# Pooled attention and a SOLU feed-forward on one core: wider loads and stores, and scores from every fourth token of a group

## The chip, the core and the metric

The kernel runs on one NeuronCore of a Trainium2 chip. Its engines work side by side, each through its own instructions in order: TensorE (PE, with PEld for its weight loads), VectorE (DVE), ScalarE (ACT), GpSimd (POOL), and SyncE (SP), which here only issues DMAs. The metric is the device time of one execution in microseconds (us), as the median of several runs.

## What is computed

Four batches of 12288 query tokens attend to 768 keys each. The keys are the means of 4x4 patches of `kv`, multiplied by a weight; they serve as values too. The result goes through a feed-forward layer with 1024 hidden units, a SOLU activation and a normalisation.

```python
r = 4
kv_pool = kv.reshape(B, H // r, r, W // r, r, C).mean(axis=(2, 4))
k = v = kv_pool.reshape(B, -1, C) @ w_sr            # 4 x 768 x 128
s = scale * (q @ k.transpose(0, 2, 1))              # 4 x 12288 x 768
a = np.exp(s - s.max(-1, keepdims=True))
a /= a.sum(-1, keepdims=True) + 1e-09
x = (a @ v).reshape(B * N, C)                       # 49152 x 128
...
h = x @ w_in                                        # 49152 x 1024
e = np.exp(h - np.max(h, axis=-1, keepdims=True))
solu = h * (e / (np.sum(e, axis=-1, keepdims=True) + 1e-09))
mu, var = mean and variance of solu over the last axis
return (((solu - mu) / np.sqrt(var + 1e-06) * g_ln) @ w_out)
```

## The kernel before

**Tiles and groups.** The 49152 tokens are 384 tiles of 128 tokens (`NT`), four tiles to a group (`GT`), 96 tiles to a batch (`TPB`). A tile's tokens lie on the 128 partitions for the scores, the hidden layer and the output. Queries arrive transposed (channels on partitions, tokens along the row), a group's 512 tokens at a time.

**Work of one tile.** Products are made from a high and a low part of each operand, so each matrix product takes three passes.

- Scores (`scores_pe`, line 402): the weights that PE loads are 128 columns of qh or ql, f32; kh and kl, 2x384 columns, stream past them: six loads and six matmuls. Line 398 picks the columns: tile j of a group takes columns j x 128 to j x 128 + 127. DVE takes the row maximum (419), ACT the exponential (420) and the high part (422), DVE the low part (430); SP issues a transposing DMA phl -> pT (433).
- Values (`values`, 456): 18 matmuls of 512 columns a group, spread over its tiles.
- Hidden layer (`hidden_pe`, 513): six matmuls of 512 columns. DVE (521, 554), ACT (537, 604) and POOL (578, 585) make u and split it into uhl; SP issues a transposing DMA uhl -> uT (589).
- Output (`final_pe`, 629): 24 weight loads from uT, 24 matmuls of 128 columns. Each group of four tiles is scaled by DVE (653) and stored by one DMA (662): its token j x 128 + p stands on partition p, so 512 bytes of a row of the output are one run.

**Keys.** A batch's keys are the sum of 16 patch positions. For batch 0 (`kv_first_load`, 163) they are loaded in 16 pieces of 384 KB and summed in PE. For batches 1 to 3 `kv_load` (204) loads one position, 384 KB, and `kv_add` (215) adds two halves of it on POOL. `kv_plan` lays these steps, and what makes keys and values of the sum, on slots of the batch before. The tiles are tag `kvc`, nine buffers of 3072 bytes a partition; other things (`vhl`, the last tiles' `uhl`) use the same tag.

**Queries.** `q_load` (373) loads one group, 256 KB, into one of three buffers, two groups ahead; `q_split` (382, ACT) makes the high part qh and `q_low` (390, POOL) the low part ql.

**Order.** The order is written by hand. The loop over `slot` (866 to 922) issues, for each slot, steps of several tiles at different stages: scores of tile slot + 1, the exponential of tile slot, the hidden layer of a tile ten slots back, the output of a tile thirteen slots back; `hidden_turn` of a tile comes eleven slots after its scores and `final_pe` two slots later. POOL's steps of the plan (`kv_add`) and SP's (`kv_load`) come at the end of a slot. All loads, stores and transposes go through SP's one queue in this order. Before the loop the loads of batch 0's keys, of both weights, of the first queries and of the first positions of batch 1 (`SOON`) are issued; the loop's table `SOON` also gave the slots of these positions' additions.

Of the kernel before, what the change touches and what calls it, by code (L numbers as in the profile page):

```python
# [11 lines left out]
F32 = mybir.dt.float32  # L12
F32R = mybir.dt.float32r
F16 = mybir.dt.float16
# [7 lines left out]
P = 128  # L22
B = 4
NTOK = 12288
NK = 768
RR = 16
DFF = 1024
# [4 lines left out]
GT = 4  # L32
# [22 lines left out]
IN_AT = 0  # L55
OUT_AT = 4

SOON = {0: (), 1: (-1, -1), 2: (8, 9), 3: (20, 22), 4: (24, 26), 5: (28, 30), 6: (32, 36)}
OUT0 = 6


# [1 line left out]
def kernel(  # L63
# [15 lines left out]
    nc = tc.nc  # L79

    dmt = ctx.enter_context(tc.tile_pool(name="dmt", bufs=2))
# [56 lines left out]
    state = {}  # L138
# [16 lines left out]
    def half_of(name, b, half):  # L155
        return state[name, b][:, half * 384 : half * 384 + 384]

    def kv_first_load(half, c):

        n = half * 8 + c  # L160
        tag, bufs = ("kvc", 9) if n < 9 else ("uT", 4) if n < 13 else ("uhl", 3)
        t = dmt.tile([P, 2, 384], F32, tag=tag, name=f"kv_{half}_{c}", bufs=bufs)
        nc.sync.dma_start(t, kv0[:, 2 * c : 2 * c + 2, half * 384 : half * 384 + 384])
        state["kv0", half, c] = t

# [31 lines left out]
        )  # L197
        nc.scalar.copy(half_of("kT", 0, half), pk)

    def kv_load(b, pos):  # L200

        t = dmt.tile([P, 2, 384], F32, tag="kvc", name=f"kv_{b}_{pos}", bufs=9)
        r, two = divmod(pos, 2)
        nc.sync.dma_start(
            t, kv[b - 1, r, :, two * NK : (two + 1) * NK].rearrange("p (h k) -> p h k", h=2)
        )
        state["kv", b, pos] = t

    def kv_add(b, half, pos):

# [108 lines left out]

    def kv_v_high(b, half):  # L320
        if half == 0:
            state["vhl", b] = dmt.tile([P, 2, NK], F16, tag="kvc", name=f"vhl_{b}", bufs=9)
        nc.gpsimd.tensor_scalar(
            state["vhl", b][:, 0, half * 384 : half * 384 + 384],
            half_of("ks", b, half),
            1.0,
            1.0,
            op0=ALU.mult,
            op1=ALU.mult,
        )  # L330
# [14 lines left out]
    def kv_plan(b):  # L345


        for pos in range(RR):


            if b == 1 and pos in SOON:
                for half, slot in enumerate(SOON[pos]):
                    yield slot, [partial(kv_add, b, half, pos)]
                continue

            n = pos - len(SOON) if b == 1 else pos
            slot = 12 * (n // 2) + 8 * (n % 2) + (7 if b == 1 else -37)
            yield slot, [partial(kv_load, b, pos)]
            if pos:
                yield slot + 3, [partial(kv_add, b, 0, pos)]  # L360
                yield slot + 5, [partial(kv_add, b, 1, pos)]
        for slot, part, *fs in PLAN:
            yield slot, [partial(f, b, part) for f in fs]


    QL = 1

    def q_load(g):
        if g >= NG or g % QL:
            return  # L370
        b, gb = divmod(g, GPB)
        t = dmt.tile([P, QL * 512], F32, tag="qf", name=f"qf_{g}", bufs=3)
        nc.sync.dma_start(t, qT[b, :, gb * 512 : (gb + QL) * 512])
        state["qf", g // QL] = t

    def q_split(g):
        if g >= NG:
            return
        qf = state["qf", g // QL][:, (g % QL) * 512 : (g % QL + 1) * 512]
        qh = grp.tile([P, 512], F32R, tag="qh", name=f"qh_{g}")  # L380
# [4 lines left out]
    def q_low(g):  # L385
        if g >= NG:
            return
        qf = state["qf", g // QL][:, (g % QL) * 512 : (g % QL + 1) * 512]
        qh, ql = state["q", g]
# [3 lines left out]
    def scores_pe(t):  # L393
        g, j = divmod(t, GT)
        b = t // TPB
        qh, ql = state["q", g]
        kh, kl = state["kh", b], state["kl", b]
        ts = slice(j * P, (j + 1) * P)
        s = ps_r.tile([P, 2, 512], F32, tag="r", name=f"s_{t}")
        for n, (lh, rh) in enumerate(((qh, kh), (qh, kl), (ql, kh))):  # L400
            for half in range(2):
                nc.tensor.matmul(  # L402
                    s[:, half, :384],
                    lh[:, ts],
                    rh[:, half * 384 : (half + 1) * 384],
                    start=n == 0,
                    stop=n == 2,
                )
        state["s", t] = s[:, :, :384]
        state["free", t] = s  # L410
# [154 lines left out]
    def hidden_high(t):  # L565
        u, _ = state["u", t]
        if t in LOW_DVE:
            uhl = [
                dmt.tile([P, DFF], F16, tag="kvc", name=f"uhl_{t}_{a}", bufs=9) for a in range(2)
            ]  # L570
            state["uhl", t] = uhl
        else:
            state["uhl", t] = dmt.tile([P, 2, DFF], F16, tag="uhl", name=f"uhl_{t}", bufs=3)
            uhl = [state["uhl", t][:, a, :] for a in range(2)]
        if t in HIGH_ACT:
            nc.scalar.copy(uhl[0], u)  # L576
        else:
            nc.gpsimd.tensor_scalar(uhl[0], u, 1.0, 1.0, op0=ALU.mult, op1=ALU.mult)  # L578
        state["halves", t] = uhl
# [69 lines left out]
    def final_out(g, j0=0, j1=GT):  # L649
        n = j1 - j0  # L650
        _, f = state["f", g]
        ob = dmt.tile([P, n, P], F32, tag="ob", name=f"ob_{g}_{j0}")
        nc.vector.scalar_tensor_tensor(
            ob,
            state["po", g][:, j0 * P : j1 * P].rearrange("p (j c) -> p j c", j=n),
            swi,
            f[:, j0:j1].unsqueeze(2).to_broadcast([P, n, P]),
            op0=ALU.mult,
            op1=ALU.mult,
        )  # L660
        t0 = g * GT + j0
        nc.sync.dma_start(
            out[t0 * P : (t0 + n) * P, :].rearrange("(j p) c -> p j c", p=P), ob
        )


# [27 lines left out]
    for n in range(16):  # L694
        if n == IN_AT:
            nc.sync.dma_start(raw_in, w_in.bitcast(I32))
        if n == 4:
            q_load(0)
        if n == OUT_AT:
            nc.sync.dma_start(raw_out, w_out.bitcast(I32))  # L700
        kv_first_load(*divmod(n, 8))
    if OUT_AT == 16:
        nc.sync.dma_start(raw_out, w_out.bitcast(I32))
    q_load(1)
    for pos in SOON:
        kv_load(1, pos)
    nc.scalar.mul(w_sr16, wsr, 1.0 / RR)

    wf, wr, in_steps = float64_parts(raw_in, "in")
# [95 lines left out]
    def w_low():  # L805
# [4 lines left out]
        1: [w_sum, partial(kv_norm_max, 0, 0)],  # L810
        2: [partial(kv_scale_v, 0, 1), partial(kv_scale_v, 0, 2), partial(kv_now, 0, kv_vs),
            partial(kv_now, 0, kv_v_high), partial(kv_now, 0, kv_v_low)],
        3: [partial(kv_norm_max, 0, 1), w_scale],
        4: [partial(kv_v_turn, 0, 0), w_in_low],
# [19 lines left out]
        (84, 0, kv_bound), (87, 1, kv_bound), (88, 2, kv_bound),  # L834
        (89, 0, kv_vs), (90, 1, kv_vs),
        (91, 0, kv_v_high), (92, 0, kv_v_low), (93, 1, kv_v_high), (94, 1, kv_v_low),
        (95, 0, kv_v_turn),
    ]
# [20 lines left out]
    for b in range(1, B):  # L859
        for k, fs in kv_plan(b):  # L860
            plan.setdefault((b - 1) * TPB + k, []).append(fs)
    for st in plan.pop(-1):
        st[0]()
    taken = []
    scores_pe(0)
    for slot in range(NT):

# [18 lines left out]
        if 0 <= av < NG:  # L886
            values(av, qtr, 0)
        at(slot + 1, scores_pe)
        for st in todo + [[partial(f, 0, 0) for f in (kv_norm_pe, kv_norm_out)]] * (slot == 4):
            if len(st) == 2:  # L890
                st[0](state["free", slot + 1])
                taken.append(st[1])
        at_soon(slot - NORM, values_norm)
        at_last(slot - FSC, final_scale)
        at(h0, hidden_high)
        at(h0, hidden_low)
        at_last(slot - FSC, final_root)
# [16 lines left out]
        if slot % GT == 0:  # L914
            q_load(slot // GT + 2)
        at_last(slot - LO - 1, final_out)
        at_soon(slot - XSP, values_out)
        for st in todo:
# [8 lines left out]
    for i in range(NT - LH, NT + 1):  # L927
        k = i - (NT - LH)
        if k in (0, XH):
            g = G - 1 if k == 0 else G  # L930
# [12 lines left out]
        if i - OB < LAST - GT:  # L943
            at_last(i - OB, final_out)
# [3 lines left out]
        if i < LAST:  # L948
            hidden_high(i - 1)
            hidden_low(i - 1)  # L950
            if i < LAST - 1:
                hidden_var(i - 1)
        elif i == LAST:
            hidden_high(i - 1)
            hidden_turn_half(i - 1, 0)
# [17 lines left out]
    final_scale(G)  # L973
    final_root(G)
    final_out(G - 1)
    for t in range(LAST - 1, LAST + 1):
        final_pe(t)
# [38 lines left out]
```

## Time and profile before

| | |
|---|---|
| median of 3 runs | 1879.23 us (1876.52 to 1888.96) |
| profiled execution | 1880.71 us, its span 1878.9 us |
| chain of work that ended last, by engine | PE 66%, POOL 11%, DVE 10%, issue 6%, DMA 4%, ACT 3% |
| DMA packets | 1483748, 434.43 MB; 1411472 of them under 512 bytes |
| HBM | 52.50 MB read, 25.17 MB written |
| L629 PEld, idle until DMA uT<-uhl | 35.3 us, 39 times |

The times of the prediction are made against the profiled execution. Busy time of an engine is a share of the span over stages with different limits; what a stage costs is read from a window of that stage. Rows of windows give the length of a window, then the busy time and the number of instructions (x) of each engine, the clock that TensorE was granted (1.00 is full), the share of the 16 DMA engines (overlapping packets count twice, so it goes above 1), and GB/s. Rows of waits give the engine and line that waited, what for, the total, the times and the longest. Rows of a timeline give start, length, engine, line, operation, the tile written and read, and how many instructions are merged.

### The profile page before, as it was taken

What the parts mean: (1) busy time and instruction counts of PE and PEld (TensorE: products, weight loads), DVE (VectorE), ACT (ScalarE), POOL (GpSimd) and SP (SyncE); (2) the same over time, 40 slices, a digit from 0 to 9 for tenths busy, and PEclk for the clock granted to TensorE, in tenths of its full rate; (3) what the DMA queues carried; (4) which work ended last, traced back from release to release, by engine and by line L of the source; (5) the groups of instructions that cost most, each with busy time, mean ns of one, the idle gap of its engine ahead of it and who ended that gap; (6) DMA issues with size and microseconds to landing.
All of it is one profiled execution on the core that took longest, in us unless ns stands there. A gap on an engine that the chain in (4) does not pass through costs nothing.

```text
span 1878.9 us, 43063 instructions
## 1 busy us (share of the span) xinstructions
PE 1837.0 (98%) x15676; PEld 1296.2 (69%) x15676; DVE 1787.7 (95%) x2692; ACT 1751.8 (93%) x3136; POOL 1630.9 (87%) x1400
## 2 busy tenths in 40 slices
PE   7899999999999999999999999999999999999997
PEld 5566777676676767767667767776677777777775
DVE  7899999999999999999999999999999999999996
ACT  4899999999999999999999999999999999999997
POOL 5899998999989888899988988888898888888886
PEclk9999999999999999999999999999999999999999
DMA  8999999999999999999999999999999999999998
GB/s 295 196 227 232 237 237 236 230 241 237 227 248 228 237 233 241 235 235 235 242 234 239 237 233 243 242 230 220 223 227 231 226 221 229 230 223 230 218 223 161
DMA packets 1483748, 434.43 MB, mean 231 GB/s; under 512 B 1411472, under 2 KB 1464848, under 8 KB 1483280
## 3 DMA queue, kind: packets, MB, share of 16 engines
q1 hardware_dynamic: 1483248, 431.60, 114.2%
q8 instruction: 124, 2.03, 0.5%
q14 instruction: 88, 0.72, 0.1%
q10 hardware_dynamic: 288, 0.07, 0.0%
HBM read 52.50 MB, written 25.17 MB: 41 GB/s over the span
## 4 chain that ended last, share of the span: by engine, by line
PE 66%; POOL 11%; DVE 10%; issue 6%; DMA 4%; ACT 3%; POOLq 0%; DVEq 0%; SPq 0%; ACTq 0%
PE o L629 19%; PE h L513 18%; PE s L402 15%; PE xa L456 14%; POOL uhl L585 4%; DMA uT<-uhl 3%; POOL uhl L578 3%; DVE junkd L521 2%; DVE nm L419 2%; DVE u L554 2%; DVE phl L430 2%; POOL ka L215 1%; DVE xl L472 1%; POOL ql L390 1%; ACT e L537 1%
## 5 line engine op out<-in xcount | busy, mean ns | idle before, releaser
L585 POOL TENSOR_TENSOR uhl<-u,uhl 128x1024 f16<-128x1024 f32 x382 | 815.7, 2136 | 33.5 <-ACT uhl L576 2.1
L629 PEld LDWEIGHTS <-uT 128*128 128x128 f16 x9216 | 545.0, 98 | 108.6 <-DMA uT<-uhl 22.5
L629 PE MATMUL o<-wch,uT 128*128 128x128 f16 x6144 | 577.2, 219 | 13.9 <-DMA uT<-uhl 12.8
L629 PE MATMUL o<-wcl,uT 128*128 128x128 f16 x3072 | 533.5, 219 | 0.0
L578 POOL TENSOR_SCALAR uhl<-u 128x1024 f16<-128x1024 f32 x377 | 394.8, 1047 | 150.8 <-DVE u L554 144.7
L554 DVE SCALAR_TENSOR_TENSOR u<-h,rz,e 128x1024 f32<-128x1024 f32 x384 | 491.3, 1279 | 29.3 <-ACT e L537 18.5
L521 DVE TENSOR_SCALAR_CACHE_REDUCE junkd<-h,rz 128x1024 bf16<-128x1024 f32 x384 | 491.1, 1279 | 4.6 <-PE h L513 4.1
L456 PE MATMUL xa<-pT,vT 128*128 128x512 f16 x1728 | 484.1, 381 | 1.7 <-DMA vT<-vhl 1.7
L537 ACT ACTIVATE e<-h,nm,rz 128x1024 f32<-128x1024 f32 x384 | 458.9, 1195 | 2.9 <-DVE junkd L521 2.9
L604 ACT ACTIVATE junk<-u,su 128x1024 bf16<-128x1024 f32 x384 | 438.1, 1141 | 0.2 <-DVE u L554 0.2
L419 DVE TENSOR_REDUCE nm<-s 128x1 f32<-128x768 f32 x384 | 364.9, 950 | 25.9 <-PE s L402 13.3
L420 ACT ACTIVATE s<-s,nm 128x768 f32<-128x768 f32 x384 | 335.4, 873 | 52.3 <-DVE nm L419 51.5
L430 DVE SCALAR_TENSOR_TENSOR phl<-s,phl 128x768 f16<-128x768 f32 x384 | 366.1, 953 | 2.5 <-ACT phl L422 2.5
L422 ACT ACTIVATE phl<-s 128x768 f16<-128x768 f32 x384 | 311.5, 811 | 14.1 <-DMA pT<-phl 2.0
L513 PEld LDWEIGHTS <-xh 128*128 128x128 f16 x1536 | 139.9, 98 | 198.3 <-DVE phl L430 31.7
L402 PE MATMUL s<-kh,qh 128*128 128x384 f32 x768 | 256.3, 415 | 9.4 <-DVE u L554 3.9
L456 PEld LDWEIGHTS <-vT 128*128 128x128 f16 x1728 | 139.5, 98 | 141.6 <-issue 57.1
L513 PE MATMUL h<-w_in_h,xh 128*128 128x512 f16 x768 | 228.7, 379 | 5.8 <-DVE phl L430 3.2
L513 PE MATMUL h<-w_in_h,xl 128*128 128x512 f16 x768 | 228.4, 379 | 0.0
L513 PE MATMUL h<-w_in_l,xh 128*128 128x512 f16 x768 | 228.4, 379 | 0.0
L402 PE MATMUL s<-kh,ql 128*128 128x384 f32 x768 | 197.0, 338 | 0.0
L402 PE MATMUL s<-kl,qh 128*128 128x384 f32 x768 | 195.1, 335 | 0.0
(121 smaller groups left out, 1686.2 us busy)
## 6 DMA issues: line engine op xcount, KB each, us to landing
kv<-in_kv_dram SPq DMA_DIRECT2D x64, 384.0 KB, 4.4
qf<-in_q_dram SPq DMA_DIRECT2D x96, 256.0 KB, 3.4
out_dram<-ob SPq DMA_DIRECT2D x95, 256.0 KB, 2.7
uT<-uhl SPq DMA_TRANSPOSE x386, 4.3
pT<-phl SPq DMA_TRANSPOSE x384, 4.0
raw_in<-in_moe_w_in_dram SPq DMA_DIRECT2D x1, 1024.0 KB, 5.2
raw_out<-in_moe_w_out_dram SPq DMA_DIRECT2D x1, 1024.0 KB, 8.0
out_dram<-ob SPq DMA_DIRECT2D x2, 128.0 KB, 1.8
```

The source lines that it names most:

```text
L402: nc.tensor.matmul(s[:, half, :384], lh[:, ts], rh[:, half * 384 : (half + 1) * 384], start=n == 0, stop=n == 2,)
L419: nc.vector.tensor_reduce(nm, s, axis=AX.XY, op=ALU.max, negate=True)
L430: nc.vector.scalar_tensor_tensor(phl[:, 1], state.pop(("s", t)), SC, phl[:, 0], op0=ALU.mult, op1=ALU.subtract)
L456: nc.tensor.matmul(xa, vT[:, v * NKC + c, :], pT[:, :, a * NKC + c, :], start=n == 0, stop=n == len(seq) - 1,)
L513: nc.tensor.matmul(h[:, hs], lh[:, ts], rh[:, hs], start=n == 0, stop=n == 2)
L521: nc.vector.tensor_scalar(junk, state["h", t], state["rz", g][1][:, j : j + 1], None, op0=ALU.mult, op1=ALU.min, accum_out=nm,)
L537: nc.scalar.activation(e, state["h", t], AF.Exp, bias=nm, scale=state["rz", g][0][:, js], accum_out=state["z2", g][:, js],)
L554: nc.vector.scalar_tensor_tensor(u, state.pop(("h", t)), state["rz", g][2][:, j : j + 1], state.pop(("e", t)), op0=ALU.mult, op1=ALU.mult, ...
L578: nc.gpsimd.tensor_scalar(uhl[0], u, 1.0, 1.0, op0=ALU.mult, op1=ALU.mult)
L585: engine.tensor_tensor(low, u, high, op=ALU.subtract)
L604: nc.scalar.activation(junk, u, AF.Square, scale=-float(DFF), bias=su, accum_out=state["v3", g][:, j : j + 1],)
L629: nc.tensor.matmul(po[:, ts], uT[:, a * NFC + c, :], w[:, c, :], start=start, stop=stop)
```

## The change

Four things change.

1. **A tile is every fourth token of its group.** `scores_pe` takes columns j, j + 4, j + 8, ... of qh and ql as weights, a step of four f32. Token 4p + j of a group then stands on partition p of tile j, from the scores to the output.
2. **The store** of a group writes the four tokens of a partition, which are neighbours in the output: 128 runs of 2048 bytes.
3. **Keys.** `kv_load` takes two positions at once, 768 KB, into five buffers of 6144 bytes a partition. Ahead of the loop four such loads (eight positions) are issued for batch 1. The plan is laid anew: batch 1's additions at slots 9 to 57, one or two slots apart; for batches 2 and 3 a load every twelve slots, its additions 2, 5, 8 and 11 slots later. Batch 0's pieces use the same tiles, two pieces to a tile.
4. **Queries.** `QL = 2`: one load of 512 KB for two groups, into one of two buffers.

```diff
-SOON = {0: (), 1: (-1, -1), 2: (8, 9), 3: (20, 22), 4: (24, 26), 5: (28, 30), 6: (32, 36)}
+SOON = 4
...
-        tag, bufs = ("kvc", 9) if n < 9 else ("uT", 4) if n < 13 else ("uhl", 3)
-        t = dmt.tile([P, 2, 384], F32, tag=tag, name=f"kv_{half}_{c}", bufs=bufs)
+        if n < 10:
+            if n % 2 == 0:
+                state["kv0", n] = dmt.tile(
+                    [P, 2, 2, 384], F32, tag="kvc", name=f"kv_{half}_{c}", bufs=5
+                )
+            t = state["kv0", n - n % 2][:, n % 2]
+        else:
+            tag, bufs = ("uT", 4) if n < 14 else ("uhl", 3)
+            t = dmt.tile([P, 2, 384], F32, tag=tag, name=f"kv_{half}_{c}", bufs=bufs)
...
-    def kv_load(b, pos):
-
-        t = dmt.tile([P, 2, 384], F32, tag="kvc", name=f"kv_{b}_{pos}", bufs=9)
-        r, two = divmod(pos, 2)
-        nc.sync.dma_start(
-            t, kv[b - 1, r, :, two * NK : (two + 1) * NK].rearrange("p (h k) -> p h k", h=2)
-        )
-        state["kv", b, pos] = t
+    def kv_load(b, r):
+
+        t = dmt.tile([P, 2, 2, 384], F32, tag="kvc", name=f"kv_{b}_{r}", bufs=5)
+        nc.sync.dma_start(t, kv[b - 1, r].rearrange("p (w h k) -> p w h k", w=2, h=2))
+        for w in range(2):
+            state["kv", b, 2 * r + w] = t[:, w]
...
-        for pos in range(RR):
-
-
-            if b == 1 and pos in SOON:
-                for half, slot in enumerate(SOON[pos]):
-                    yield slot, [partial(kv_add, b, half, pos)]
-                continue
-
-            n = pos - len(SOON) if b == 1 else pos
-            slot = 12 * (n // 2) + 8 * (n % 2) + (7 if b == 1 else -37)
-            yield slot, [partial(kv_load, b, pos)]
-            if pos:
-                yield slot + 3, [partial(kv_add, b, 0, pos)]
-                yield slot + 5, [partial(kv_add, b, 1, pos)]
+
+        for r in range(RR // 2):
+            slot = 12 * r - 42
+            if b > 1 or r >= SOON:
+                yield slot, [partial(kv_load, b, r)]
+            for n in range(4):
+                pos, half = 2 * r + n // 2, n % 2
+                if not pos:
+                    continue
+                if b > 1:
+                    at = slot + 3 * n + 2
+                elif pos == 1:
+                    at = -1
+                else:
+                    at = 9 + 9 * (4 * (r - 1) + n) // 5
+                yield at, [partial(kv_add, b, half, pos)]
...
-    QL = 1
+    QL = 2
...
-        t = dmt.tile([P, QL * 512], F32, tag="qf", name=f"qf_{g}", bufs=3)
+        t = dmt.tile([P, QL * 512], F32, tag="qf", name=f"qf_{g}", bufs=2)
...
-        ts = slice(j * P, (j + 1) * P)
+        ts = slice(j, GT * P, GT)
...
-        t0 = g * GT + j0
         nc.sync.dma_start(
-            out[t0 * P : (t0 + n) * P, :].rearrange("(j p) c -> p j c", p=P), ob
+            out[g * GT * P : (g + 1) * GT * P, :].rearrange("(p j) c -> p j c", j=GT)[:, j0:j1], ob
         )
...
-    for pos in SOON:
-        kv_load(1, pos)
+    for r in range(SOON):
+        kv_load(1, r)
```

More of the change, by code (lines that the diff above doesn't have):

```diff
@@ L321, in kv_v_high @@
         if half == 0:
-            state["vhl", b] = dmt.tile([P, 2, NK], F16, tag="kvc", name=f"vhl_{b}", bufs=9)
+            state["vhl", b] = dmt.tile([P, 2, NK], F16, tag="kvc", name=f"vhl_{b}", bufs=5)
         nc.gpsimd.tensor_scalar(
@@ L568, in hidden_high @@
             uhl = [
-                dmt.tile([P, DFF], F16, tag="kvc", name=f"uhl_{t}_{a}", bufs=9) for a in range(2)
+                dmt.tile([P, DFF], F16, tag="kvc", name=f"uhl_{t}_{a}", bufs=5) for a in range(2)
             ]
```

## The prediction

> **What bounds the kernel now.** I read the page's busy shares first, then equal amounts of work in different stages, then the chain of waits inside the quietest stage.
>
> ```profile
> span 1878.9 us, 43063 instructions
> PE 1837.0 (98%) x15676; PEld 1296.2 (69%) x15676; DVE 1787.7 (95%) x2692; ACT 1751.8 (93%) x3136; POOL 1630.9 (87%) x1400
> ...
> core 0: us, PE busy (x) PEld busy (x) DVE busy (x) ACT busy (x) POOL busy (x), PEclk, DMA share, GB/s
> 67.04:294.22 227.18, 223.26 (x1893) 156.30 (x1894) 216.52 (x320) 213.79 (x381) 208.86 (x179) 1.00 1.15 229
> 466.95:752.77 285.82, 282.05 (x2434) 199.08 (x2432) 274.02 (x406) 269.68 (x482) 254.62 (x217) 1.00 1.20 236
> 924.93:1208.03 283.10, 281.36 (x2434) 199.47 (x2432) 273.85 (x406) 269.66 (x482) 254.62 (x217) 1.00 1.20 238
> 1379.52:1660.02 280.50, 280.50 (x2434) 199.78 (x2432) 273.33 (x406) 269.39 (x482) 235.34 (x197) 1.00 1.15 227
> ```
>
> The busy shares alone decide nothing: four engines are near full. The four windows are cut at the first matmul of s of a tile. The last three each hold 60 tiles, tiles 0 to 59 of batches 1, 2 and 3, with the same 2434 matmuls; the first holds tiles 12 to 59 of batch 0. In batch 3 no keys are prepared, PE is busy 280.50 of 280.50 us, and a tile takes 280.50/60 = 4.675 us. DVE, ACT and POOL have idle time there, so PE alone sets this pace, at a granted clock of 1.00 and with the DMA engines' share above 1.
>
> ```profile
> 1444.86 0.30 PEld L402 LDWEIGHTS s<-kh,qh 128*128 128x128 f32 x2
> 1445.15 0.36 PEld L402 LDWEIGHTS s<-kl,qh 128*128 128x128 f32 x2
> 1445.50 0.36 PEld L402 LDWEIGHTS s<-kh,ql 128*128 128x128 f32 x2
> ...
> 1445.08 1.09 PE s L402 x6
> 1446.17 0.88 PE xa L456 x4
> 1447.05 1.29 PE h L513 x6
> 1448.35 1.34 PE o L629 x24
> 1449.69 0.22 PE xa L456
> ...
> 1440.75 1.04 PE s L402 x6
> ```
>
> The middle rows are the chain of waits for one tile in that stage: nothing but PE; the last is the tile before. Scores s, values xa, hidden h and output o follow each other without a gap. So whatever the change adds to a PE section is paid 384 times, and whatever it takes off the DMA queues is worth only PE's stalls elsewhere. At 4.675 us a tile, 48 tiles of batch 0 need 224.4 us. The stretches of batches 0 to 2 therefore lose 227.18 - 224.4 = 2.8, 285.82 - 280.5 = 5.3 and 283.10 - 280.5 = 2.6 us: 10.7 us in all.
>
> **The weight loads of s, read in strides.** The two multiplications with qh and the one with ql load six 128x128 f32 weights a tile. Today each partition reads 128 neighbouring f32; then it reads one f32 of every four, 16 bytes apart. The number and size of the matmuls stay. What matters is whether a slower load is still covered by the matmul before it.
>
> ```profile
> L402 PEld LDWEIGHTS s<-kl,qh x768: 186/188/331, 29.5 to 1824.1; 128*128 128x128 f32 x192
> ...
> 36.92 0.50 PEld L402 LDWEIGHTS s<-kh,qh 128*128 128x128 f32 x2 [1.20 <-PE s L402]
> ...
> 36.90:38.80 1.90, 1.85 (x6) 1.78 (x6) 1.87 (x5) 1.87 (x5) 1.23 (x2) 0.50 0.79 178
> ```
>
> The recorded 0.188 us of a load is not its cost, because loads overlap. The pairs of loads quoted above say more. In a pair of 0.36 us the second ends 0.19 us after its own start, so it started 0.36 - 0.19 = 0.17 us after the first: that is the matmuls' pace (1.04 to 1.09 us for six). The pair of 0.30 us, the first two loads of a tile whose preceding matmul is a short one of o, shows a load that nothing holds back: the next could start 0.30 - 0.19 = 0.11 us later. So a load needs about 0.11 us under a cover of 0.17.
>
> At a granted clock of 0.50 (last row) the free pair takes 0.50 us. Its second load is recorded at about 0.33 us, near the 331 ns maximum quoted, so the distance is about 0.165 us. My estimate from these two points: 0.165 - 0.11 = 0.055 us of a load is reading of columns at full clock, and 0.055 us is fixed. The half-clock row is also a direct picture of a load whose reading takes twice as long: 0.165 us, still under 0.17.
>
> No row shows a 16-byte step, so the cost is bounded. Lower end: nothing, 0 us; a gain is excluded, since PE runs at the matmuls' pace here. Upper end: today a 16-byte piece serves four columns, then one; if each piece costs what it costs now, reading takes 4 x 0.055 = 0.22 us and a load 0.275. Then five loads of a tile each add 0.275 - 0.17 = 0.105. The first, behind a 0.22 us matmul of xa in three tiles of four, adds 0.055, and behind a short one of o in the fourth 0.275 - 0.11 = 0.165. A tile pays 0.525 + 0.75 x 0.055 + 0.25 x 0.165 = 0.61 us, and 384 tiles 233 us. At twice the reading time only the fourth tile's first load shows: 0.25 x 0.055 x 384 = 5.3 us. The cover is gone at (0.17 - 0.055)/0.055 = 2.1 times.
>
> ```profile
> L712 DVE TENSOR_SCALAR ex_in<-ex_in 128x1024 int32<-128x1024 int32 x3 | 2.1, 691 | 0.1
> L712 DVE TENSOR_SCALAR ex_in<-raw_in 128x1024 int32<-128x1024 int32 x1 | 0.7, 694 | 4.7 <-DMA raw_in<-in_moe_w_in_dram 4.7
> ```
>
> The nearest strided row is DVE's: ex_in<-raw_in takes every second 32-bit word, 8 bytes apart, in 694 ns; the same operation on neighbouring words takes 691. Half-used pieces cost nothing there. It is another engine and half the step, so I take the lower part of the range: between no loss and twice the reading, **+3 us** (ends 0 and +233).
>
> The Trainium skill, Advanced Engine Details and Errata (Memory Cachelines, SBUF Cachelines), speaks against this: it puts SBUF lines at 16 bytes, wants at least two hits on a line to absorb the access latency, and names a penalty for a different line on each access. By it the DVE row (two hits, 691 against 694 ns) should be free, and the trace agrees; the one hit of the new loads no run here shows. It gives no size for PE. With the P / 1.2 of TensorE: Matmul & The Clock Gate (LDWEIGHTS (loading the stationary operand)), 107 ns for 128 columns, doubled to 213 as an estimate, a tile would pay about 0.24 us and the kernel about 92 us.
>
> **Stores of 2048 bytes.** A group's 512 tokens then lie four to a partition, so a store writes 128 runs of 2048 bytes instead of 512 of 512. The same bytes move, with fewer descriptors.
>
> ```profile
> kv<-in_kv_dram SPq DMA_DIRECT2D x64, 384.0 KB, 4.4
> qf<-in_q_dram SPq DMA_DIRECT2D x96, 256.0 KB, 3.4
> out_dram<-ob SPq DMA_DIRECT2D x95, 256.0 KB, 2.7
> ...
> PEld L629 <- DMA uT<-uhl: 14.2, 20, 1.8
> PE o L629 <- DMA uT<-uhl: 5.7, 10, 1.4
> ```
>
> Nobody waits for a store; its queue is shared with the transposes uT, for which PE waited 14.2 + 5.7 us between 160 and 1830 us (the two waits rows). Batch 3 does the same stores without a stall, so relief there is worth nothing. In the measured stretches at most the 10.7 us lost in batches 0 to 2 can return: ends -10.7 and 0. Most of that loss comes where keys are loaded and added, so I take **-4 us**.
>
> **Keys of two positions in a load.** 24 loads of 768 KB replace 48 of 384 KB for batches 1 to 3, and the additions keep their number and size. Batch 1's first eight positions are asked for ahead of the loop (seven today), and its remaining additions are spread over tiles 9 to 57; the four later loads are issued 24, 19, 15 and 10 tiles before their first addition, so POOL cannot wait for them unless they are very late. In batches 2 and 3 the first addition follows its load by two tiles instead of three, in seven pairs of eight (the first pair has eight).
>
> ```profile
> 647.32 0.57 SPq L204 DMA_DIRECT2D kv<-in_kv_dram  x1
> ...
> 656.84 1.01 POOL L215 TENSOR_TENSOR ka<-ka,kv 128x384 f32<-128x384 f32 x1
> ```
>
> From issue to first addition are 656.84 - 647.32 = 9.5 us today; one tile less leaves 4.85. Loads of 256 and 384 KB land after 3.4 and 4.4 us, so 768 KB after about 3.4 + 4 x 1.0 = 7.4 (estimate): each of 14 additions would hold POOL about 2.5 us, and behind it wait the splits of u into uhl, their transposes, and PE's o. POOL is idle 285.82 - 254.62 = 31.2 us in 60 tiles, 0.52 a tile, and 12 tiles lie between loads, so each delay is made good in some five tiles. Ends: 0 and 14 x 2.5 = +35 us; I take **+3 us**, a tenth, since o comes about two tiles after its transpose is issued and that slack takes most of it. Should the estimate of the landing be too long, the wait is gone altogether.
>
> **Queries of two groups in a load.** 48 loads of 512 KB for 96; they are issued five tiles before their first use, as now, and the two double buffers come free as early as the three single ones. In the loop nothing waits. At the start 256 KB more stand before 12 of batch 0's key loads:
>
> ```profile
> 5.96 11.43 SPq L163 DMA_DIRECT2D kv<-in_kv_dram  x12
> ...
> PE pk L179 <- DMA kv<-in_kv_dram: 7.1, 1, 7.1
> ```
>
> Twelve loads of 384 KB took 11.43 us, so 256 KB are 0.65 us. PE waited for these loads only once, before the first matmul, and that load is still ahead of the queries; taken 0, ends 0 and +0.65. SP issues 24 + 48 = 72 loads fewer at about 0.57 us, 41 us of its queue; since batch 3 runs with PE never waiting, taken 0.
>
> **Sum.** The profiled execution took 1880.71 us (span 1878.9 and 1.8 around it), against a median of 1879.23. 1880.71 + 3 - 4 + 3 = 1882.7, so 1883 us, 0.2% above the median. About 1% is what a measurement of this kernel can tell from no change (1860 to 1898).
>
> **The rivals.** *A load of s outgrows its cover* (slower). Place: the six loads of L402. It decides from 2.1 times the reading time on: 0.006 us over the cover on five loads, with the fourth tile's first load, is already 1%. For it: no gap in PE, so nothing absorbs it, and the step leaves a piece of 16 bytes with one use. (The rule of the Trainium skill's Advanced Engine Details and Errata, Memory Cachelines, quoted above, is this mechanism.) Against it: 0.165 us at twice the reading is still covered, and DVE's 8-byte step is free. Between 2.1 and 4 times it gives 1885 to 2114; its middle is 2000 us.
>
> *The wider key load is late at POOL.* All 14 waits reach PE: 1883 + 32 = 1915 us. For it: 4.85 us of lead against an estimated 7.4. Against: POOL's 0.52 us a tile, and o's distance from its transpose.
>
> *The DMA relief returns more than the stretches show:* the whole wait for uT, 14.2 + 5.7 = 19.9 us, goes: about 1861 us. Against: that sum includes delays that come from POOL, not from the queue.
>
> **How the numbers follow.** Forecast 0.46 (its own range 1868 to 1897); the load over its cover 0.44; the late key load 0.07; full relief 0.03. The range 1866 to 2050 leaves out the relief and those loads above 3.5 times the reading, 0.15. Faster by over 1%: the relief, 0.03. Slower: 0.41 of the covered-load rival (0.03 of it stays under 1898) and half the late key load, 0.45. Within 1%: the rest, 0.52.
>
> **What would show it.** If the loads are covered, batch 3's 60 tiles still take 280.5 us and six matmuls of s 1.04 to 1.09. If not, that row grows to 1.2 to 1.7 us, every other PE section keeps its length, and DVE, ACT and POOL get idle time. Pairs of loads of 0.30 us would read 0.36 at twice the reading. A late key load would show as POOL idle before L215's additions. The prediction is wrong if the s row grows by more than 0.05 us a tile, or if PE's stalls in batches 1 and 2 exceed today's 5.3 and 2.6 us by some ten.

## The result and the profile after

The changed kernel takes 1990.54 us (median, 1989.61 to 1991.51) against 1881.09 for the kernel before in the same runs: 1.0577 times as long, 95% interval 1.0558 to 1.0596. The point forecast, 1883 us, was wrong by 107 us and had the wrong verdict; the time lies inside the stated range because of the first rival.

The page of the changed kernel, its first lines and the chain that ended last:

```profile
span 1989.7 us, 42994 instructions
PE 1961.6 (99%) x15676; PEld 1468.0 (74%) x15676; DVE 1801.6 (91%) x2692; ACT 1757.1 (88%) x3136; POOL 1631.6 (82%) x1400
...
PE 95%; ACT 1%; DMA 1%; DVE 1%; issue 1%; POOL 0%; SPq 0%; POOLq 0%; DVEq 0%; ACTq 0%
PE s L409 26%; PE o L636 25%; PE h L520 24%; PE xa L463 19%; DMA kv<-in_kv_dram 1%; ACT e L544 0%; PE pk L186 0%; ACT junk L611 0%; DMA vT<-vhl 0%; DVE phl L437 0%; POOL kv L183 0%; DVE u L561 0%; PE s L226 0%; ACT uhl L583 0%; DVE junkd L528 0%
```

PE's share of the chain rose from 66% to 95%, and the scores are now its costliest line. The count of instructions on PE is unchanged, 15676. The same stretches as before, tiles 0 to 59 of batches 1, 2 and 3 (length, then busy time of PE, PEld, DVE, ACT, POOL, clock, DMA share, GB/s):

```profile
491.36:792.46 301.10, 301.10 (x2434) 226.37 (x2432) 275.99 (x406) 270.18 (x481) 253.59 (x215) 1.00 1.12 224
974.75:1275.85 301.10, 301.10 (x2434) 226.36 (x2432) 275.99 (x406) 270.18 (x481) 253.63 (x215) 1.00 1.13 225
1457.92:1759.02 301.10, 301.10 (x2434) 226.35 (x2432) 275.98 (x406) 270.18 (x481) 235.62 (x196) 1.00 1.04 212
```

Two things are to be seen. A tile takes 301.10/60 = 5.018 us instead of 4.675, 0.343 more, at the same granted clock. And all three stretches are equal to a hundredth: the stalls that batches 1 and 2 had before (5.3 and 2.6 us) are gone; between 160 and 1830 us the trace has no wait of PE for a transpose left. Over 384 tiles 0.343 us are 132 us; the spans differ by 1989.7 - 1878.9 = 110.8. About 21 us of stalls were given back. 12.6 of them lie in the stretches of the prediction: tiles 12 to 59 of batch 0 grew by 238.99 - 227.18 = 11.8 instead of 16.5 us, and the others by 15.3 and 18.0 instead of 20.6.

Where the 0.343 us are, in batch 3 (the weight loads of a tile that follows a short matmul of o, then the chain of the tiles around it):

```profile
1507.95 0.54 PEld L409 LDWEIGHTS s<-kh,qh 128*128 128x128 f32 x2
1508.40 0.56 PEld L409 LDWEIGHTS s<-kl,qh 128*128 128x128 f32 x2
1508.86 0.56 PEld L409 LDWEIGHTS s<-kh,ql 128*128 128x128 f32 x2
...
1503.52 1.36 PE s L409 x6
1504.87 0.66 PE xa L463 x3
1505.54 1.29 PE h L520 x6
1506.83 1.34 PE o L636 x24
1508.17 1.51 PE s L409 x6
1509.68 0.88 PE xa L463 x4
...
L409 PEld LDWEIGHTS s<-kl,qh 128*128 128x128 f32 x768 | 216.6, 330 | 0.0
```

Only the s row grew, from 1.04 and 1.09 us to 1.36 and 1.51; h, o and a matmul of xa keep their 1.29, 1.34 and 0.22. A load is recorded at 0.33 us (last row). So in the pair of 0.54 the second starts 0.54 - 0.33 = 0.21 us after the first, where it was 0.11: that is what a strided load needs when nothing holds it. In the pairs of 0.56 the distance is 0.23 us, where the matmuls' pace was 0.17. Five such distances, 0.06 us more each, and the first load's part (0.02 us behind a matmul of xa, 0.11 behind one of o) make the 0.34 us. Why the distance between the matmuls of s is 0.02 us longer than that of the unheld pair, no run shows.

### The profile page after: what moved, and what is told of

The parts are those of the page before. It is cut to its first block, busy times and chain, and to the rows that moved or that the text cites. A ratio compares the mean times of both kernels' runs of the same rounds, so it can differ in the third digit from the quotient of the medians.

```text
span 1989.7 us, 42994 instructions
## 1 busy us (share of the span) xinstructions
PE 1961.6 (99%) x15676; PEld 1468.0 (74%) x15676; DVE 1801.6 (91%) x2692; ACT 1757.1 (88%) x3136; POOL 1631.6 (82%) x1400
## 4 chain that ended last, share of the span: by engine, by line
PE 95%; ACT 1%; DMA 1%; DVE 1%; issue 1%; POOL 0%; SPq 0%; POOLq 0%; DVEq 0%; ACTq 0%
PE s L409 26%; PE o L636 25%; PE h L520 24%; PE xa L463 19%; DMA kv<-in_kv_dram 1%; ACT e L544 0%; PE pk L186 0%; ACT junk L611 0%; DMA vT<-vhl 0%; DVE phl L437 0%; POOL kv L183 0%; DVE u L561 0%; PE s L226 0%; ACT uhl L583 0%; DVE junkd L528 0%
## 5 line engine op out<-in xcount | busy, mean ns | idle before, releaser
L409 PE MATMUL s<-kh,qh 128*128 128x384 f32 x768 | 298.1, 470 | 4.4 <-DVE phl L437 2.6
L520 PEld LDWEIGHTS <-xh 128*128 128x128 f16 x1536 | 149.7, 98 | 183.5 <-DVE phl L437 2.9
L409 PE MATMUL s<-kl,qh 128*128 128x384 f32 x768 | 242.7, 398 | 0.0
L409 PE MATMUL s<-kh,ql 128*128 128x384 f32 x768 | 242.3, 398 | 0.0
```

What stands on the lines that cost most here:

```text
L409: nc.tensor.matmul(s[:, half, :384], lh[:, ts], rh[:, half * 384 : (half + 1) * 384], start=n == 0, stop=n == 2,)
L520: nc.tensor.matmul(h[:, hs], lh[:, ts], rh[:, hs], start=n == 0, stop=n == 2)
```

## The experiments

All ratios are to the kernel before, run beside it on the same chip.

**1. The strides alone.** In the kernel before, one line:

```diff
-        ts = slice(j * P, (j + 1) * P)
+        ts = slice(j, GT * P, GT)
```

> The kernel before with one line changed: scores take columns j, j + 4, ... as weights; the store stays as it was, so the rows of the output stand permuted within each group. Theory (the strided load alone makes the loss): two loads of s that nothing holds start 0.21 us apart instead of 0.11, the six matmuls of s keep 0.233 us instead of 0.172, a tile in batch 3 takes 5.02 us instead of 4.675, and the time is 1985 to 1995 us. Rival (half or more of the loss comes from the wider loads, the stores or the new plan): under 1940 us.

Measured: 1992.0 us (ratio 1.059, 1.0569 to 1.0612), the time of the whole change. Its stretches of batches 1 and 3:

```profile
489.51:790.61 301.10, 301.10 (x2434) 226.34 (x2432) 275.97 (x406) 270.19 (x481) 254.48 (x217) 1.00 1.10 226
1455.84:1756.94 301.10, 301.10 (x2434) 226.32 (x2432) 275.98 (x406) 270.17 (x481) 235.65 (x196) 1.00 1.05 212
```

The same 301.10 us, in batch 2 too. One line makes the loss; the loads, stores and plan add nothing beside it.

**2. The rest alone.** The changed kernel, with the permutation of tokens moved into the layout of the queries on the host:

```diff
-        ts = slice(j, GT * P, GT)
+        ts = slice(j * P, (j + 1) * P)
...
-        "q": inputs["q"].transpose(0, 2, 1),
+        "q": inputs["q"].reshape(B, GPB, P, GT, P).transpose(0, 4, 1, 3, 2).reshape(B, P, NTOK),
```

> The changed kernel with contiguous weights: the queries are laid out on the host with the tokens of a group in the order of the tiles, so tile j takes columns 128j to 128j + 127 and these still are every fourth token; stores, key loads, query loads and plan as changed. Theory (these parts are hidden): batch 3 runs at 4.675 us a tile again, and the time is 1868 to 1885 us, below the kernel before by at most the 11 us that its batches 0 to 2 lose. Rival (the late key load): 1890 to 1915 us, with POOL waiting for DMA before its additions in batches 1 and 2.

Measured: 1895.4 us (1.0087, 1.0056 to 1.0118), inside the rival's 1890 to 1915. The 95 us between this run and the changed kernel are the strides; the rest is not hidden either, but costs about 14 us where PE has its old pace. Batch 3 is back at 4.675 us a tile, batches 1 and 2 lose 9.2 and 9.9 us (5.3 and 2.6 in the kernel before), and new waits stand in the list (waiter, releaser, total us, times, longest):

```profile
470.13:759.84 289.71, 283.58 (x2434) 200.00 (x2432) 274.39 (x406) 270.12 (x483) 253.87 (x216) 0.99 1.19 232
1397.64:1678.15 280.51, 280.51 (x2434) 199.73 (x2432) 273.28 (x406) 269.18 (x482) 235.09 (x197) 1.00 1.13 228
...
POOL ka L220 <- DMA kv<-in_kv_dram: 20.3, 9, 4.1
PE xa L463 <- DMA pT<-phl: 12.2, 8, 2.8
```

How a wide load reaches PE, in one place (SP's queue, then POOL, then the chain of work that ended last):

```profile
685.60 0.57 SPq L210 DMA_DIRECT2D kv<-in_kv_dram  x1
686.27 1.39 SPq L440 DMA_TRANSPOSE pT<-phl  x1
687.76 5.02 SPq L596 DMA_TRANSPOSE uT<-uhl  x1
692.88 1.42 SPq L440 DMA_TRANSPOSE pT<-phl  x1
...
685.73 2.14 POOL L592 TENSOR_TENSOR uhl<-u,uhl 128x1024 f16<-128x1024 f32 x1
691.66 0.99 POOL L220 TENSOR_TENSOR ka<-ka,kv 128x384 f32<-128x384 f32 x1 [3.80 <-DMA kv<-in_kv_dram]
...
686.27 6.91 DMA pT<-phl
693.17 0.25 issue
693.42 1.65 PE xa L463 x4
```

POOL stands 3.80 us, until the load has landed at about 691.6. But PE's wait does not come from POOL. It ends with the transpose that was issued at 686.27, right behind the load: it lands after 6.91 us, where the median of these transposes is 3.9. All eight waits in the row of pT above are of this kind; the transpose behind the wide load landed 6.5 to 8.1 us after its issue. The next transpose, of uhl, then stays at the head of SP's queue for 5.02 us. POOL is not what holds it, since POOL's part of uhl was ready at 685.73 + 2.14 = 687.87. What does hold it is not shown; it moves on when the transpose before it has nearly landed.

**3. A step of two columns.** As the changed kernel, but tile j takes every second token of half a group:

```diff
-        ts = slice(j, GT * P, GT)
+        ts = slice(j // 2 * 2 * P + j % 2, (j // 2 + 1) * 2 * P, 2)
...
-            out[g * GT * P : (g + 1) * GT * P, :].rearrange("(p j) c -> p j c", j=GT)[:, j0:j1], ob
+            out[(g * GT + j0) * P : (g * GT + j1) * P, :].rearrange("(h p i) c -> p h (i c)", p=P, i=2),
+            ob.rearrange("p (h i) c -> p h (i c)", i=2),
```

> The changed kernel with a step of two f32 (8 bytes) in the weights of s: tile j takes every second token of one half of its group, and a store writes runs of 1024 bytes; the result is the reference's. Theory (what costs is that a 16-byte piece serves a single column): two columns a piece are enough, the unheld load stays near 0.11 us (0.16 at most), the matmuls of s keep 0.172 us, and the time is that of the run with contiguous weights, 1868 to 1885 us. Rival (any step of more than one column slows the load, in proportion to the span it reads): a load of 0.16 us or more and 0.18 to 0.20 us between matmuls, 1900 to 1940 us.

Measured: 1901.2 us (1.0104, 1.0079 to 1.013), which its interval cannot tell from experiment 2. The time missed the stated 1868 to 1885, because experiment 2 did, and by itself would even fit the rival's 1900 to 1940. PE's own pace decides, and it is as the theory had it:

```profile
1504.08 0.32 PEld L409 LDWEIGHTS s<-kh,qh 128*128 128x128 f32 x2
1504.38 0.37 PEld L409 LDWEIGHTS s<-kl,qh 128*128 128x128 f32 x2
...
L409 PEld LDWEIGHTS s<-kl,qh 128*128 128x128 f32 x768 | 143.0, 196 | 0.3 <-DVE kl L197 0.3
...
1400.99:1682.07 281.08, 281.04 (x2434) 201.40 (x2432) 273.34 (x406) 269.21 (x482) 235.16 (x197) 1.00 1.16 226
```

Unheld distance 0.32 - 0.20 = 0.12 us, pace 0.37 - 0.20 = 0.17, and 281.08 us for 60 tiles, 0.01 us a tile more than with no step. An 8-byte step is all but free here.

**4. A longer cover.** The changed kernel, with matmuls of xa (512 columns, 0.216 us) put between those of s in three tiles of four:

```diff
+                if between:
+                    between.pop(0)()
...
-        at(slot + 1, scores_pe)
+        mixed = 2 <= av < NG and qtr > 0 and slot + 1 < NT
+        at(slot + 1, scores_pe, values(av, qtr, 1, True) if mixed else ())
```

> The changed kernel, strides and all, with the order of PE changed: in three tiles of four the three or four matmuls of xa that followed the scores now stand one each between the matmuls of s; the result is the reference's. Theory (the load outgrows the 0.172 us of the matmul before it, and that is all): behind a matmul of xa of 0.216 us a load of 0.211 is covered, so 11 of the 20 loads in four tiles no longer add 0.061 us; four tiles take 20.07 - 0.67 = 19.4 us, and the kernel loses some 64 us: 1920 to 1930 us. Rival (a matmul of s with strided weights is itself slower, 0.233 us whatever stands before it): four tiles keep 20.07 us and the time stays 1985 to 1995 us.

Measured: 1975.5 us (1.0511, 1.0492 to 1.0529): both numbers missed, one by some 50 us and the other by 10. The chain, the window of batch 3, and the matmuls of two tiles show why it must be read in two parts:

```profile
1506.65 0.21 PE xa L466
1506.87 0.19 PE s L410
1507.05 0.23 PE xa L466
1507.29 0.18 PE s L410
...
1446.81:1745.26 298.45, 298.03 (x2434) 223.32 (x2432) 273.32 (x406) 271.31 (x481) 235.71 (x197) 1.00 1.06 214
...
1513.05 0.63 PE L410 MATMUL s<-kh,ql 128*128 128x384 f32 x2
1513.52 0.61 PE L528 MATMUL h<-w_in_h,xh 128*128 128x512 f16 x2
...
1517.69 1.04 PE L466 MATMUL xa<-pT,vT 128*128 128x512 f16 x4
1518.75 0.59 PE L528 MATMUL h<-w_in_h,xh 128*128 128x512 f16 x2
...
1518.61 0.12 DVE rz L510
1518.75 1.46 PE h L528 x6
```

Behind a matmul of xa, a strided s takes 0.18 us, not 0.23, and the pair 0.41 instead of 0.23 + 0.22 = 0.45: the load is all but covered (0.17 + 0.22 = 0.39 would be full cover), and the matmul itself is not slower. The rival falls at this row.

But only 2.65 us came off batch 3 (298.45 against 301.10 in 60 tiles), 0.18 us in four tiles instead of the expected 0.67. The recorded ends of the matmuls in the trace say where the rest is. In four tiles, eleven matmuls of s that now follow one of xa save 0.05 us each, 0.55 in all. Eleven matmuls, eight of xa and three of h, now follow one of s and take 0.016 us longer each for it, as a matmul of xa behind s did before (0.232 us against 0.216): 0.18 is lost again. And in the one tile whose scores were left as they were, the first matmul of h comes 0.19 us late. It starts only at 1518.75, after the last matmul of xa has ended and after rz of DVE, where the h of the tile before starts while the last s still runs. 0.55 - 0.18 - 0.19 = 0.18. The mechanism was right and the price of the new order was not seen.

**5. A step of three columns**, tiles overlapping as its expectation says:

```diff
-        ts = slice(j, GT * P, GT)
+        ts = slice(j, j + 3 * P - 2, 3)
```

> The changed kernel with a step of three f32 (12 bytes) in the weights of s: the tile's tokens are j, j + 3, ... of its group, so that tokens overlap between tiles and rows of the output belong to others. Three 16-byte pieces then serve four columns. Theory (a piece costs about 0.21 / 128 = 1.65 ns, a column with a used piece half of that): an unheld load of about 0.16 us, under its cover of 0.172, so 5.02 us a tile fall back to 4.68 to 4.72. Rival (any step beyond two columns pays in full): 0.21 us and 5.02 us a tile.

```profile
1516.80 0.43 PEld L409 LDWEIGHTS s<-kh,qh 128*128 128x128 f32 x2
...
L409 PEld LDWEIGHTS s<-kl,qh 128*128 128x128 f32 x768 | 166.5, 254 | 0.2 <-DVE kl L197 0.2
...
1394.33:1677.23 282.90, 282.90 (x2434) 208.12 (x2432) 274.63 (x406) 270.05 (x481) 235.30 (x197) 1.00 1.15 225
```

In the trace the pair of the first row lasts 0.427 us and its second load 0.263 (the mean of 254 ns in the next row is of other loads), so the unheld distance is 0.427 - 0.263 = 0.16 us, as expected. 282.90/60 = 4.715 us a tile is the upper edge of what was expected. The whole took 1898.7 us in a single run, with the key waits of experiment 2 in it.

The four steps form one line. The 128 columns lie in 32, 64, 96 and 128 pieces of 16 bytes; the unheld load takes 0.11, 0.12, 0.16 and 0.21 us. The last two are some 1.7 ns a piece, and at 64 pieces and below the load is near its least, 0.11. Up to this step the pieces and the bytes that the load spans grow together, so these runs cannot say which of the two is paid for; a step of 20 bytes, with 128 pieces and a longer span, would.

**6. The rest, taken apart.** Three versions. In the first, on top of experiment 2, key loads of batches 2 and 3 go out two tiles earlier:

```diff
-            slot = 12 * r - 42
+            slot = 12 * r - 44 if b > 1 else 12 * r - 42
...
-                    at = slot + 3 * n + 2
+                    at = slot + 3 * n + 4
```

> The run with contiguous weights and all the rest of the change, but for batches 2 and 3 each wide key load is issued two tiles earlier; its additions stay where they are, so the first follows its load by four tiles instead of two. Theory (the 14 us by which that run was slower than the kernel before come from the additions waiting for their load): POOL's 20.3 us of waiting for key loads go to under 3, the stalls of 4 us in batches 1 and 2 go, and the time is 1872 to 1884 us. Rival (the long loads hold up the transposes behind them on the DMA queue, whenever they are issued): 1888 to 1897 us with no wait at POOL.

Measured: 1885.8 us (1.0019, 1.0005 to 1.0033), 2 us above the theory's range and 2 below the rival's. POOL's wait for key loads in the loop is gone, and 12.2 us of PE's wait for pT became 2.6. So some 10 of the 14 us are gone.

```profile
670.28 0.43 SPq L210 DMA_DIRECT2D kv<-in_kv_dram  x1
670.81 2.95 SPq L440 DMA_TRANSPOSE pT<-phl  x1
673.86 4.62 SPq L596 DMA_TRANSPOSE uT<-uhl  x1
```

The late additions are not thereby shown to be the cause, since the edit changes two things. With no wait at POOL the transpose behind a wide load still lands 6.1 to 10.0 us after its issue, and SP still stays 4.0 to 6.6 us on the one of uhl (4.62 in the last row), so POOL caused neither. But a load at slot 12r - 42 stands ahead of the scores' transpose of the last tile of a group, and two slots earlier ahead of that of the second tile. xa of a group reads the pT of all four tiles, so the delayed transpose now has two tiles more. The longest wait for pT that is left, 2.4 us, is behind a load of batch 1, which the edit did not move. The 9.6 us that PE's wait for pT lost are the size of the gain; what POOL's wait added to it, if anything, is not separated. PE's waits for uT have even grown, to 27.2 us on PEld and 17.7 on PE from 22.5 and 12.8 in the kernel before (the 35.3 us of its table are both together), and the wide loads bring nothing even when they are early.

The second is the kernel before with the host's permutation, wide stores and wide query loads, keys untouched:

> The kernel before, with the tokens permuted on the host, stores in runs of 2048 bytes, and queries of two groups in a load; keys as before. Theory (keys alone cost): 1868 to 1881 us. Rival (the wider query loads hold up the transposes too): above 1884 us, and above the run with the stores alone by 4 us or more.

Measured: 1883.5 us (1.0007, 0.9993 to 1.0021), between the two expectations: no gain, and 5 us above the next version. Whether the wide query loads cost these 5 us is not settled; the intervals just touch.

The third has only the permutation and the stores:

```diff
-            out[t0 * P : (t0 + n) * P, :].rearrange("(j p) c -> p j c", p=P), ob
+            out[g * GT * P : (g + 1) * GT * P, :].rearrange("(p j) c -> p j c", j=GT)[:, j0:j1], ob
```

> The kernel before, with the tokens permuted on the host and stores in runs of 2048 bytes; queries and keys as before. PE's work is that of before. Theory (stores have no one waiting, and the relief of the DMA queue is small): 1870 to 1881 us, of the 11 us lost in batches 0 to 2 some 0 to 5 return. Rival (the relief of the queue is worth more): under 1870 us.

Measured: 1878.6 us (0.998, 0.9967 to 0.9993). It is faster than the kernel before by 0.2%. The time that the host takes for the permutation is not part of the metric.

## Why the prediction was wrong, step by step

**The bound: right.** PE sets the pace with no gap in batch 3, and whatever a PE section gains is paid 384 times. The measured 0.343 us a tile appear in every stretch.

**The weight loads of s: the step that failed.** The prediction held that "the half-clock row is also a direct picture of a load whose reading takes twice as long", split the 0.11 us of a load into 0.055 fixed and 0.055 of reading, and took the lower part of the range, +3 us. The runs do not bear the split out: over 96 and 128 pieces the load takes some 1.7 ns for each, with 0.11 us as its least. At the step of four it takes 0.21 us, over the 0.17 of its cover, where the split gave 0.165 for twice the reading. The half clock and the step in memory slow a load by different amounts, 0.165 and 0.21 us, and the one was taken for the other.

The same step erred in picking its nearest row. DVE's 8-byte step, free at 694 against 691 ns, was right for 8 bytes on PE too (experiment 3), but said nothing of 16, where a piece serves one column. The upper end, 0.61 us a tile, held: the measured 0.343 lies between the ends. The rival named the mechanism; that its 2000 us came near is in part luck, since it was the middle of a range and no sum of its own.

The Trainium skill's Advanced Engine Details and Errata (Memory Cachelines, SBUF Cachelines), which the prediction weighed and set aside, was the better guide: it wants at least two hits on a 16-byte line. The traces agree: with two hits the unheld load takes 0.12 us (experiment 3), with one 0.21 (experiment 1). The Trainium skill's TensorE: Matmul & The Clock Gate (LDWEIGHTS (loading the stationary operand)) gives a load of P columns P / 1.2 ns, 107 for 128. The 0.11 us of the kernel before agrees. The prediction's doubling of it to 213 was an estimate, and met the unheld load of 0.21. It gave 92 us and not 132, because next to the matmuls of s the distance is 0.23 and not 0.21: some 0.02 us more on each of five loads.

**Stores: nearly the right size, the mechanism not seen.** Taken -4, measured -2.6 us (ratio 0.998) by themselves. The trace kept of this version does not show the relief: PE's waits for uT are 13.8 us on PEld and 5.1 on PE (14.2 and 5.7 before), and the 60 tiles of batches 1 and 2 took 283.89 and 284.86 us, together what they took before (285.82 and 283.10). It cannot exclude it either, since it is of the slowest execution of the version, 1883.2 us. The third rival's 14.2 + 5.7 = 19.9 us also counted stops twice, where a weight load and the matmul after it waited for one transpose (0.98 and 0.49 us at 508.82, for example).

**Keys: the waits at POOL as foretold, the path to PE wrong.** The estimate had 14 additions wait 2.5 us each; nine waits came to 20.3 us, 2.3 each. But PE's new stalls do not come through POOL, u and o. They come from the scores' transpose that stands right behind the wide load in SP's queue and lands late with it, for which the prediction had no term. Of the 14 us of experiment 2, moving the loads took back some 10, where 3 had been taken for the additions. In the changed kernel the transposes behind the wide loads land as late (5.8 to 8.7 us after their issue), but PE, slower by 0.34 us a tile, waits for none of them in the loop.

**Queries: taken 0; open within 5 us** (experiment 6).

**Sum.** +3 for the loads should have been +132, less about 21 us of stalls that a slower PE covers. That give-back was in no term of the sum.

## What to carry to other kernels

A covered load has a margin, and the margin has to be compared with what the new access pattern costs, which here went with the step in bytes while the number of elements stayed the same. If a layout has to be permuted, permute it where no engine on the path reads with a step (here on the host, whose time is not measured); 8 bytes was still all but free where 16 was not. A slower clock in a trace is no stand-in for a slower memory access. And before a load is made wider, look at what stands behind it in the same queue and how soon that is needed: the transpose behind it was late whether or not anyone waited for the load itself.

## What the runs showed of the hardware

An f32 weight load of 128 columns that nothing holds takes 0.11, 0.12, 0.16 and 0.21 us at steps of 4, 8, 12 and 16 bytes. Between matmuls of 384 columns the distance stays at 0.17 us up to 8 bytes, is 0.18 at 12 and 0.23 at 16. A transpose of scores right behind a load of 768 KB in SP's queue landed 6.4 to 9.1 us after its issue in experiment 2, where their median is 3.9. Steps beyond 16 bytes, and f16 weights with a step, were not tried.
